# Decode attention on one core: output weights in longer rows with selection matmuls, and the last keys and values in smaller loads

## Chip, cores and metric

The kernel runs on 1 core of one Trainium2 chip. The metric is device time in microseconds (us) of one execution.

## The reference, cut to what matters

Two attention layers decode one new token for a batch of 4, and their outputs are concatenated. The model width is D = 512, and a head has 128 elements.

```python
# A: 32 query heads share 8 key/value heads; only the last W = 2048 of 8192 keys count
W = min(4096, max(256, Sk // 4))
k = jnp.repeat(k_cache[:, :, Sk - W:, :], 4, axis=1)      # v likewise
# B: 32 heads, each with its own 8192 keys
scores = einsum("bhqd,bhkd->bhqk", x @ wq, k) * Dh ** -0.5
o = einsum("bhqk,bhkd->bhqd", softmax(scores), v)
out = o.reshape(B, 1, 32 * 128) @ wo
return concatenate([a, b], axis=-1)
```

The caches are what costs: 32 MB of them are read for A (8 chunks of 2 MB of keys and 2 MB of values), 512 MB for B. Each element is used once, so this is a problem of loading.

## The kernel before

Work is cut into chunks. An A chunk is one key/value head for all four batches: 2 MB of keys and 2 MB of values. There are 8 of them. A B chunk is two heads of one batch: 4 MB and 4 MB, and there are 64. PE (the matmul engine) transposes the keys in groups of 8 tiles, multiplies them with the queries, and in the next chunk multiplies the values with the softmax weights. The DVE (vector) and ACT (scalar) engines copy the transposed keys out of PSUM, the memory into which PE writes, and do the softmax in between.

```python
def keys_part(c):
    for g in range(ch["NG"]):                 # 8 groups in A, 16 in B
        emit_T(ch["s"] + g)                   # 8 transposes, then a copy to SBUF on DVE or ACT
        if g >= SLAG:
            emit_S(ch["s"] + g - SLAG)        # scores, two groups behind
        if 1 <= c < NCA and g == 2: stats_gmax(c - 1)     # softmax of the chunk before:
        if 1 <= c < NCA and g == 3: stats_exp(c - 1)      # max, shift, exp, row sums
        if 1 <= c < NCA and g == 6: norm_sum(c - 1)
        if 2 <= c < NCA and g == 4: emit_fin(c - 2)       # output projection of A
        ...
        if c >= NCA and c % 2 == 1 and g == 10: emit_fin(ahead(c, 2))   # of B
```

One queue issues the loads in the order of use. A load waits for the buffer that it fills. The output weights of a group of heads are loaded with one weight row of 512 elements (1 KB) per descriptor.

```python
def dma_wo(g):                                # A: 512 KB per chunk, 8 of them
    src = A_wo[g * 4 * P:(g + 1) * 4 * P, :].rearrange("(hl d) n -> d hl n", d=P)
    ...
def dma_wos(hp):                              # B: 256 KB per head pair, 16 of them
    src = B_wo[2 * hp * P:2 * (hp + 1) * P, :].rearrange("(hl d) n -> d hl n", d=P)
```

## Time and profile before

| | before |
|---|---|
| time, three runs | 1381.89 us median (1379.97 to 1385.78) |
| profiled run | 1380.14 us, span 1378.3 us |
| PE busy | 1174.6 us (85%) |
| DVE busy, ACT busy | 641.7 us (47%), 436.0 us (32%) |
| DMA | 587.53 MB, mean 426 GB/s |
| packets under 2 KB | 10992 of 30085 |

The DMA engines have work from the first slice of the span to the last, and PE is busy 85% of it, over three stages: A (from about 34 us, when the first scores are done, to about 116 us), B (to 1352 us) and a tail without loads that matter. The distance between two landings is what a load costs the stream, and the distance between two like instructions of successive chunks (the chunk period) is what a chunk costs the engines. The period in A, read from the starts of the first softmax instruction of each chunk (the group `sA<-sc,mk`), is 11.16 us before. The stream of loads is read from the landings of A's weights, one load per chunk: they are 11.27 to 11.32 us apart (about 4.9 us for the keys, 4.95 for the values and 1.44 for the weights). So these two are within 0.15 us of each other.

### The profile page before, as it was taken

How to read it: one execution, taken by the hardware profiler on the slowest of the kernel's cores; microseconds unless marked ns; L12 is line 12 of the kernel's file. 1: busy time of each engine (PE TensorE's matmuls, PEld its weight loads, DVE VectorE, ACT ScalarE, POOL GpSimd, SP SyncE). 2: the span in 40 equal slices, each digit the busy share in tenths (PEclk: the TensorE clock that was granted, in tenths of full speed). 3: DMA queues.
4: the chain of work that ended last, by engine and by line, in shares of the span. 5: the costliest groups of instructions: out<-in, count | busy, mean ns of one | idle time of the engine just before them, and what ended most of it. 6: DMA issues, size and time to landing. Idle time of an engine off the chain costs nothing.

```text
span 1378.3 us, 59408 instructions
## 1 busy us (share of the span) xinstructions
PE 1174.6 (85%) x26901; PEld 1132.8 (82%) x26901; DVE 641.7 (47%) x1337; ACT 436.0 (32%) x649; POOL 4.8 (0%) x18
## 2 busy tenths in 40 slices
PE   4887898888888888888889888988898888888988
PEld 4776898888888887888888888888898888888987
DVE  1665454444444444444444444444454445444543
ACT  1553233323223322332233232322333233332332
POOL 1000000000000000000000000000000000000000
PEclk9999999999999999999999999999999999999998
DMA  9999999999999999999999999999999999999997
GB/s 400 414 417 425 428 432 429 431 432 430 433 430 434 428 432 431 431 432 430 432 429 433 431 432 432 430 430 432 431 431 433 428 433 432 431 431 431 430 431 315
DMA packets 30085, 587.53 MB, mean 426 GB/s; under 512 B 2784, under 2 KB 10992, under 8 KB 11248
## 3 DMA queue, kind: packets, MB, share of 16 engines
q1 hardware_dynamic: 30040, 587.22, 99.6%
q8 instruction: 16, 0.26, 0.1%
q14 instruction: 5, 0.04, 0.0%
q10 hardware_dynamic: 24, 0.01, 0.0%
HBM read 587.21 MB, written 0.01 MB: 426 GB/s over the span
## 4 chain that ended last, share of the span: by engine, by line
DMA 60%; PE 37%; DVE 1%; issue 1%; ACT 0%; SPq 0%; DVEq 0%; ACTq 0%
DMA kv<-in_B_k_cache_dram 58%; PE tr L375 23%; PE sc L377 10%; PE po L377 3%; DMA kv<-in_B_wq_dram 2%; PE fin L377 2%; PE ms L377 1%; DVE sA L488 1%; DVE kt L439 0%; DVE sA L486 0%; ACT pba L551 0%; PE ms L375 0%; SPq L330 0%; SPq L314 0%; ACT kt L437 0%
## 5 line engine op out<-in xcount | busy, mean ns | idle before, releaser
L375 PE MATMUL tr<-identb,kv 128*128 128x128 bf16 x8704 | 703.5, 232 | 160.6 <-DMA kv<-in_B_k_cache_dram 158.2
L439 DVE COPY kt<-tr 128x1024 bf16<-128x1024 bf16 x736 | 503.5, 691 | 469.6 <-PE tr L375 468.6
L375 PEld LDWEIGHTS tr<-identb,kv 128*128 128x128 bf16 x8704 | 559.2, 105 | 185.7 <-DMA kv<-in_B_k_cache_dram 103.5
L437 ACT ACTIVATE kt<-tr 128x1024 bf16<-128x1024 bf16 x352 | 360.2, 1024 | 629.8 <-PE tr L375 628.9
L377 PE MATMUL sc<-qb,kt 128*128 128x64 bf16 x8704 | 446.9, 196 | 10.6 <-DVE kt L439 10.3
L377 PEld LDWEIGHTS sc<-qb,kt 128*128 128x128 bf16 x8704 | 369.3, 100 | 14.5 <-DVE kt L439 11.6
L377 PE MATMUL po<-pbb,kv 128*128 128x64 bf16 (+1 forms) x8320 | 293.8, 191 | 7.0 <-issue 7.0
L377 PEld LDWEIGHTS po<-pbb,kv 128*128 128x128 bf16 x8320 | 266.8, 97 | 9.1 <-issue 7.3
L536 ACT ACTIVATE pbb<-sc,negb 64x128 bf16<-64x128 f32 x128 | 51.2, 400 | 295.2 <-DVE negb L526 294.4
L502 DVE TENSOR_REDUCE rm<-sc 64x1 f32<-64x128 f32 x128 | 37.0, 289 | 93.1 <-PE sc L377 92.2
L514 DVE TENSOR_REDUCE gm<-ms 1x2 f32<-1x128 f32 (+1 forms) x72 | 20.1, 279 | 44.5 <-PE ms L375 44.4
L526 DVE COPY negb<-ms 128x1 f32<-128x1 f32 (+1 forms) x72 | 11.4, 159 | 55.4 <-PE ms L377 55.4
L377 PE MATMUL ms<-identf,gx 1*128 1x1 f32 (+1 forms) x144 | 27.2, 256 | 0.0
L377 PEld LDWEIGHTS ms<-identf,gx 1*128 1x128 f32 (+1 forms) x144 | 21.1, 182 | 4.5 <-DVE gx L518 0.4
L536 ACT ACTIVATION_READ_ACCUMULATOR pbb<-sc,negb 64x1 f32 x128 | 23.7, 185 | 0.0
L375 PE MATMUL ms<-identf,rm 128*1 128x128 f32 (+1 forms) x72 | 19.5, 271 | 2.3 <-DVE rm L497 2.3
L377 PE MATMUL po<-pba,kv 128*128 128x64 bf16 x512 | 20.1, 199 | 0.5 <-ACT pba L551 0.5
L377 PE MATMUL fin<-wos,oz 128*4 128x512 bf16 x66 | 20.0, 385 | 0.3 <-DVE oz L616 0.3
L377 PEld LDWEIGHTS po<-pba,kv 128*128 128x128 bf16 x512 | 17.9, 102 | 0.6 <-ACT pba L551 0.6
L518 DVE TENSOR_SCALAR gx<-gm 1x128 f32<-1x128 f32 (+1 forms) x72 | 15.9, 221 | 2.7 <-DVE gm L514 0.2
L377 PE MATMUL ms<-xT,kv 128*128 128x4 bf16 x256 | 7.1, 166 | 8.5 <-DMA kv<-in_A_wq_dram 4.4
L377 PEld LDWEIGHTS ms<-xT,kv 128*128 128x128 bf16 x256 | 7.0, 104 | 8.7 <-DMA kv<-in_A_wq_dram 4.5
(46 smaller groups left out, 136.0 us busy)
## 6 DMA issues: line engine op xcount, KB each, us to landing
kv<-in_B_k_cache_dram SPq DMA_DIRECT2D x64, 4096.0 KB, 27.3
kv<-in_B_v_cache_dram SPq DMA_DIRECT2D x63, 4096.0 KB, 32.0
kv<-in_A_k_cache_dram SPq DMA_DIRECT2D x8, 2048.0 KB, 14.0
kv<-in_A_v_cache_dram SPq DMA_DIRECT2D x8, 2048.0 KB, 16.2
kv<-in_A_wq_dram SPq DMA_DIRECT2D x1, 4096.0 KB, 12.3
kv<-in_B_wq_dram SPq DMA_DIRECT2D x1, 4096.0 KB, 27.2
wor<-in_A_wo_dram SPq DMA_DIRECT2D x8, 512.0 KB, 11.3
wos<-in_B_wo_dram SPq DMA_DIRECT2D x16, 256.0 KB, 20.8
```

The costliest lines, as they stand in the source:

```text
L375: sch.add("pe", lambda e: e.transpose(o, l, r), waits, key)
L377: sch.add("pe", lambda e: e.matmul(o, l, r, start=start, stop=stop), waits, key)
L437: sch.add("act", lambda e: e.activation(dst, src, ACTF.Copy), waits=waits, key=("ev", s))
L439: sch.add("dve", lambda e: e.tensor_copy(dst, src), waits=waits, key=("ev", s))
L488: emit = lambda e, src=src, b=b: e.scalar_tensor_tensor(out=t, in0=src, scalar=mk[:, b:b + 1], in1=t, op0=ALU.mult, op1=ALU.add)
L502: sch.add("dve", lambda e, src=src, pp=pp: e.tensor_reduce(out=rm[pp, m, 0:1], in_=src, axis=AX.X, op=ALU.max), waits=[("S", ch["s_last"]) ...
L514: sch.add("dve", lambda e: e.tensor_reduce(out=gm[0:C, m, 0:U], in_=src, axis=AX.X, op=ALU.max), waits=[("trm", c)], key=("gmax", c))
L518: sch.add("dve", lambda e: e.tensor_scalar(out=dst, in0=gv, scalar1=-scale, scalar2=None, op0=ALU.mult), waits=[("gmax", c)], key=("gx", c))
L526: sch.add("dve", lambda e: e.tensor_copy(negb[:, m, 0:C], ms[:, col:col + C]), waits=[("bc", c)], key=("negb", c))
L536: sch.add("act", lambda e, src=src, pp=pp, n=n, u=u: e.activation(pbv[pp, :, u], src, ACTF.Exp, bias=negb[pp, m, 0:1], scale=scale, accum_ ...
```

## The change

The intent has two parts. First, fewer short packets: a partition takes four (A) or two (B) neighbouring weight rows as one row of 4 or 2 KB. The rows then lie in another order than the attention output, so the output is permuted by selection matmuls and copied before the projection. Second, a shorter tail: the last keys come in two halves, so that PE can start on the first, and the last value pieces are smaller. For the last chunk the weights are turned back by a matmul, so that no selection stands in the tail.

```diff
-LASTV = (64, 32, 16, 16)
+LASTV = (64, 32, 16, 8, 8)
 ...                                  # dma_wo (A); dma_wos (B) likewise with r=2
-            src = A_wo[...].rearrange("(hl d) n -> d hl n", d=P)
+            src = A_wo[...].rearrange("(p r) n -> p (r n)", r=4)
 ...                                  # last keys in halves
+            if kind == "k" and c == NC - 1:
+                x = slice(0, NTB // 2 * P), slice(NTB // 2 * P, NTB * P)
+                sch.add_dma("sp", ... dst[:, x[0]], src[:, x[0]] ..., key=(kind, c))
+                sch.add_dma("sp", ... dst[:, x[1]], src[:, x[1]] ..., key="kl")
 ...                                  # emit_T: the second half is awaited in mid-chunk
+                    if c >= NCA and c % 2 == 1 and g == NTB // TG // 2:
+                        waits += [("wos2", ahead(c, 2))]
 ...                                  # last values with 64 columns
-                n = NW if c < NC - 1 else UC
+                n = NW
 ...                                  # the selection: k = 4 in A, 2 in B
+        def emit_sel(c):
+            for r in range(k):
+                pe_mm(ms[:, Z0 + r * n:...], sel[:, r, :], x, waits=[("oT", c)] + ms_read ...)
+            for h in range(k):
+                sch.add("dve", ... tensor_copy(z[pp, :]..., src), waits=[("sm", c)] + free ...)
+            ms_read[:] = [("z", c)]
 ...                                  # keys_part
                 if 2 <= c < NCA and g == 4:
+                    emit_sel(c - 2)
+                if 2 <= c < NCA and g == 7:
                     emit_fin(c - 2)
+                if c >= NCA and c % 2 == 1 and g == 8:
+                    emit_sel(ahead(c, 2))
 ...                                  # before the last values
         norm_sum(NC - 1)
+        emit_wol()                    # 4 matmuls with 512 columns, two copies
```

In `keys_part`, A's projection goes from the fifth group to the eighth, to leave time for the selection. At the end of A (`finish_A`, not shown) two selections are put in, and one projection is moved behind the exponential there too.

More of the change, by code (lines that the diff above doesn't have):

```diff
@@ L22 @@
 NW = 64
-LASTV = (64, 32, 16, 16)
+LASTV = (64, 32, 16, 8, 8)
 TRM0, BC0, L0, Q0, XT0 = 0, 256, 288, 320, 448
+Z0 = Q0
 class _Record:
@@ L240, in bass_concat_heads__sliding_block_cached__mha_block_cached__decode_kernel @@
         outsb = sb("outsb", [36, DO], BF16)
+        sel4 = sb("sel4", [P, 4, P], BF16)
+        sel2 = sb("sel2", [P, 2, P], BF16)
+        back2 = sb("back2", [P, 2, 2, P], BF16)
+        zA = sb("zA", [P, 2, 16], BF16)
+        zB = sb("zB", [P, 8], BF16)
+        wol = sb("wol", [P, 2, DO], BF16)
         tr = ps("tr", [P, NTRB, TG * P], BF16)
@@ L249, in bass_concat_heads__sliding_block_cached__mha_block_cached__decode_kernel @@
         semnames += ["d_h%d" % i for i in range(NH)] + ["d_vl%d" % i for i in range(len(LASTV))]
-        semnames += ["d_wo%d" % i for i in range(NWO)] + ["d_wos"]
+        semnames += ["d_wo%d" % i for i in range(NWO)] + ["d_wos", "d_kl"]
         sems = {n: es.enter_context(nc.semaphore(n)) for n in semnames}
@@ L274, in bass_concat_heads__sliding_block_cached__mha_block_cached__decode_kernel @@
         sch.add("pool", lambda e: e.memset(pbt[1][:, :, :], 0.0), key=("c_pb", 1))
+        for r in range(4):
+            sch.add("pool", lambda e, r=r: e.affine_select(
+                out=sel4[:, r, :], in_=onesb[:, :], pattern=[[0, 4], [-4, 32]], compare_op=ALU.is_equal,
+                fill=0.0, base=-r, channel_multiplier=1), waits=["c_onesb"])
+        for r in range(2):
+            sch.add("pool", lambda e, r=r: e.affine_select(
+                out=sel2[:, r, :], in_=onesb[:, :], pattern=[[0, 2], [-2, 64]], compare_op=ALU.is_equal,
+                fill=0.0, base=-r, channel_multiplier=1))
+            for u in range(2):
+                sch.add("pool", lambda e, r=r, u=u: e.affine_select(
+                    out=back2[:, u, r, :], in_=onesb[:, :], pattern=[[1, P]], compare_op=ALU.is_equal,
+                    fill=0.0, base=P * u - r, channel_multiplier=-2), key="c_sel" if r == u == 1 else None)
         half_of = {}
@@ L304, in dma_wo @@
         def dma_wo(g):
-            src = A_wo[g * 4 * P:(g + 1) * 4 * P, :].rearrange("(hl d) n -> d hl n", d=P)
+            src = A_wo[g * 4 * P:(g + 1) * 4 * P, :].rearrange("(p r) n -> p (r n)", r=4)
             slot = wo_slot(g)
-            dst = wor[:, slot, :].rearrange("p (hl n) -> p hl n", hl=4)
+            dst = wor[:, slot, :]
             sch.add_dma("sp", lambda e: e.dma_start(dst, src), "d_wo%d" % slot,
@@ L311, in dma_wos @@
         def dma_wos(hp):
-            src = B_wo[2 * hp * P:2 * (hp + 1) * P, :].rearrange("(hl d) n -> d hl n", d=P)
-            sch.add_dma("sp", lambda e: e.dma_start(wos[:, :, :], src), "d_wos",
+            src = B_wo[2 * hp * P:2 * (hp + 1) * P, :].rearrange("(p r) n -> p (r n)", r=2)
+            sch.add_dma("sp", lambda e: e.dma_start(wos[:, :, :].rearrange("p r n -> p (r n)"), src), "d_wos",
                         waits=[("fin", NCA + 4 * hp - 1)] if hp else [], key=("wos", hp))
@@ L341, in dma_kv @@
                 return
+            if kind == "k" and c == NC - 1:
+                x = slice(0, NTB // 2 * P), slice(NTB // 2 * P, NTB * P)
+                sch.add_dma("sp", lambda e: e.dma_start(dst[:, x[0]], src[:, x[0]]), "d_h%d" % at, waits=waits, key=(kind, c))
+                sch.add_dma("sp", lambda e: e.dma_start(dst[:, x[1]], src[:, x[1]]), "d_kl", key="kl")
+                return
             sch.add_dma("sp", lambda e: e.dma_start(dst, src), "d_h%d" % at, waits=waits, key=(kind, c))
@@ L361, in bass_concat_heads__sliding_block_cached__mha_block_cached__decode_kernel @@
                 hp = max(0, c - NCA - 2) // 4
-                sch.add("sp", lambda e: e.sem_inc(sems["eng_sp"], 1), waits=[("wos", hp)],
+                sch.add("sp", lambda e: e.sem_inc(sems["eng_sp"], 1), waits=[("wos", hp)] + (["kl"] if c == NC - 1 else []),
                         key=("wos2", c - 2 if c > NCA + 1 else NONE), self_inc=True)
@@ L417, in tile_of, with ahead @@
             return flat(at, chunks[c]["NT"] // NTA)[:, j * P:(j + 1) * P]
+        def ahead(c, n):
+            return c - n if c - n >= NCA else NONE
         bank_used = [None] * NTRB
@@ L614, in norm_out, with emit_wol @@
                 i1 = rz[:, :].rearrange("p (x y) -> p x y", x=2)
-            waits = [("rinv" if 0 <= c < NCA else "rz", c), ("pv", c)] + ([("fin", c - 2 if c != NCA + 1 else NONE)] if c >= 2 else [])
+            waits = [("rinv" if 0 <= c < NCA else "rz", c), ("pv", c)] + ([("sm", c - 2 if c != NCA + 1 else NONE)] if c >= 2 else [])
             sch.add("dve", lambda e: e.tensor_tensor(out=o, in0=i0, in1=i1, op=ALU.mult), waits=waits, key=("oT", c))
             po_read[:] = [("oT", c)]
+        def emit_sel(c):
+            if 0 <= c < NCA:
+                sel, x, n, z, k = sel4, oT[:, c % NSM, :], 16, zA[:, c % 2, :], 4
+                free = [("fin", c - 2)] if c >= 2 else []
+            else:
+                sel, x, n, z, k = sel2, oz[:, :], 8, zB[:, :], 2
+                free = [("fin", c - 2 if c - 2 >= NCA else NONE)] if c != NONE else []
+            for r in range(k):
+                pe_mm(ms[:, Z0 + r * n:Z0 + (r + 1) * n], sel[:, r, :], x,
+                      waits=[("oT", c)] + ms_read if r == 0 else [], key=("sm", c) if r == k - 1 else None)
+            for h in range(k):
+                pp = slice(h * P // k, (h + 1) * P // k)
+                src = ms[pp, Z0:Z0 + k * n].rearrange("p (r b h) -> p h r b", r=k, b=NB)[:, h]
+                sch.add("dve", lambda e, src=src, pp=pp: e.tensor_copy(z[pp, :].rearrange("p (r b) -> p r b", r=k), src),
+                        waits=[("sm", c)] + free if h == 0 else [], key=("z", c) if h == k - 1 else None)
+            ms_read[:] = [("z", c)]
+        def emit_wol():
+            for u in range(2):
+                o = tr[:, u, :].bitcast(F32)
+                for r in range(2):
+                    pe_mm(o, back2[:, u, r, :], wos[:, r, :], start=r == 0, stop=r == 1,
+                          waits=[("wos2", NC - 1)] if u == r == 0 else [], key=("back", u) if r else None)
+                if u == 0:
+                    sch.add("act", lambda e, o=o: e.activation(wol[:, 0, :], o, ACTF.Copy), waits=[("back", 0)], key=("wol", 0))
+                else:
+                    sch.add("dve", lambda e, o=o: e.tensor_copy(wol[:, 1, :], o), waits=[("back", 1)], key=("wol", 1))
         def emit_fin(c):
@@ L621, in emit_fin @@
             p0 = 0 if ab == 1 else 32
-            if ab == 1:
+            if c == NC - 1:
                 ov = oz[:, :].rearrange("p (b u) -> p b u", u=2)
-                ops = [(ov[:, :, u], wos[:, u, :]) for u in range(2)]
-                waits = [("oT", c), ("wos2", c)]
-            else:
-                w = wor[:, wo_slot(c), :].rearrange("p (hl n) -> p hl n", hl=4)
-                ov = oT[:, c % NSM, :].rearrange("p (u c) -> p u c", c=REP)
-                ops = [(ov[:, :, cc], w[:, cc, :]) for cc in range(REP)]
-                waits = [("oT", c), ("wo", c)]
+                ops = [(ov[:, :, u], wol[:, u, :]) for u in range(2)]
+                waits = [("oT", c), ("wol", 0), ("wol", 1)]
+            elif ab == 1:
+                ops = [(zB[:, r * NB:(r + 1) * NB], wos[:, r, :]) for r in range(2)]
+                waits = [("z", c), ("wos2", c)]
+            else:
+                w = wor[:, wo_slot(c), :].rearrange("p (r n) -> p r n", r=4)
+                ops = [(zA[:, c % 2, r * NB:(r + 1) * NB], w[:, r, :]) for r in range(4)]
+                waits = [("z", c), ("wo", c)]
             lastc = NC - 1 if ab == 1 else NCA - 1
@@ L644, in pv_done @@
                 norm_out(c)
-        def ahead(c, n):
-            return c - n if c - n >= NCA else NONE
         def keys_part(c):
@@ L699, in finish_A @@
             stats_gmax(NCA - 1)
+            emit_sel(NCA - 2)
+            stats_exp(NCA - 1)
             emit_fin(NCA - 2)
-            stats_exp(NCA - 1)
             norm_sum(NCA - 1)
@@ L705, in finish_A @@
             pv_done(NCA - 1)
+            emit_sel(NCA - 1)
             emit_fin(NCA - 1)
@@ L717, in bass_concat_heads__sliding_block_cached__mha_block_cached__decode_kernel @@
                 emit_q(1)
-                pe_mm(fin[0:36, :], pbt[0][:, 1, 0:36], pbt[0][:, 1, 0:DO], stop=False, waits=[("c_pb", 1)])
+                pe_mm(fin[0:36, :], pbt[0][:, 1, 0:36], pbt[0][:, 1, 0:DO], stop=False, waits=["c_sel"])
             values_part(None if c == 0 else NONE if c == NCA else c - 1, c)
```

## The prediction

> **What bounds the kernel now.** I read the page first (slices, queues, chain), then the DMA packet records and the landing times, then the chain of waits and the timeline of the last 40 us. The slices:
>
> ```profile
> PE   4887898888888888888889888988898888888988
> ...
> DMA  9999999999999999999999999999999999999997
> GB/s 400 414 417 425 428 432 429 431 432 430 433 430 434 428 432 431 431 432 430 432 429 433 431 432 432 430 430 432 431 431 433 428 433 432 431 431 431 430 431 315
> DMA packets 30085, 587.53 MB, mean 426 GB/s; under 512 B 2784, under 2 KB 10992, under 8 KB 11248
> ```
>
> The DMA engines are full from the first slice to the last; PE is not. So the span is a DMA stream of fixed bytes (587 MB, near 431 GB/s once problem B streams) plus what PE still does after the last loads. The early slices are slower, 400 to 428 GB/s: that is problem A, with most of the short rows. Of the 10992 packets under 2 KB, 8208 are of 1 KB, and 8192 of these are the output weights (8 loads of 512 KB and 16 of 256 KB).
>
> A load has landed when its semaphore has had the increments of all 16 engines. As loads follow each other without a gap, the distance of two landings is what the later one costs the stream. For loads of 128 rows, eight rows per engine, the trace gives 9.71 us for 32 KB rows, 4.89 for 16 KB, 2.47 for 8 KB and 1.23 to 1.24 for 4 KB (the last three are pieces of the last value chunk). Output weights in 1 KB rows cost 1.40 to 1.47 us per 512 KB (A) and 0.73 per 256 KB (B), and the load before a B one is late by another 0.02 to 0.03. Per packet that is 1214, 611, 309, 154 and, for 1 KB, 45 ns: about 37.8 ns per KB and 3 to 8 ns on top.
>
> The end, as the chain of waits has it:
>
> ```profile
> 1325.21 27.14 DMA kv<-in_B_k_cache_dram
> 1352.34 0.05 issue
> 1352.39 1.90 PE tr L375 x24
> ...
> 1365.21 0.70 PE po L377 x24
> ...
> 1370.82 0.38 PE ms L377 x2
> 1371.20 3.26 PE po L377 x128
> ...
> 1374.77 1.03 PE fin L377 x2
> 1375.80 0.02 issue
> 1375.82 0.68 DVE outsb L636
> ```
>
> The last keys land at 1352.34. From there to the end nothing waits for DMA: transposes and scores to 1365.21, the values of the last chunk but one with the softmax steps to 1371.20, the last values to 1374.46, projection, copy, store. The last value piece landed at 1371.89, before its 16 tiles were due (1371.20 + 112 x 0.0255 = 1374.06). So **the tail hangs on the landing of the last keys**, and two lines of the timeline show what PE did before them:
>
> ```profile
> 1349.02 0.41 PE L377 MATMUL po<-pbb,kv 128*128 128x64 bf16 x8
> ...
> 1352.39 1.90 PE L375 MATMUL tr<-identb,kv 128*128 128x128 bf16 x24 [2.96 <-DMA kv<-in_B_k_cache_dram]
> ```
>
> PE was idle for 2.96 us, then ran on half clock: the granted clock is 0.50 from 1353.35 to 1356.76, and eight transposes take 0.85 us there, 0.45 later.
>
> **The Trainium skill.** "DMA: Bandwidth & Descriptors", section "Why small descriptors are slow (HBM only)", says that each packet carries a fixed overhead of a few cycles and each descriptor a fixed amount of metadata. The trace agrees: 45 ns for 1 KB against 38 per KB in the longest rows. Its "Specifications" give 435 GB/s as the fabric's ceiling; the 431 here is next to it, so only overhead is left to gain. "TensorE: Matmul & The Clock Gate", Part 1, says that a free-running window of about 3.4 us decides on half clock after idling. The trace agrees: half-clock stretches last 3.41 us or multiples, and sorting this trace's windows by PE's idle time, those idle for over 2.1 us are followed by half clock, those idle for 1.64 to 1.84 (nine) are not. The same page, "Back-to-back issue gap", gives a floor of some 25 ns between small matmuls; the trace has 25.5 ns with 2 columns (3.26/128) and 29.2 with 64 (0.70/24).
>
> **The change, part by part.** (1) *Rows.* A's weights go from 1 KB to 4 KB rows. 128 rows of 4 KB is the very shape of the last value piece, 1.235 us: 8 x (1.44 - 1.235) = 1.6 us off the stream. B's go to 128 rows of 2 KB; between 1 and 4 KB the ladder gives about 82 ns a packet, 8 x 82 = 0.66 us, against 0.73 + 0.02: 16 x 0.09 = 1.4 us. Splitting the last keys adds 2 x 4.89 - 9.71 = 0.07, the smaller value pieces 2 x 0.66 - 1.235 = 0.08. Because the stream is full throughout, I count all of it on the path: **-2.9 us**, and every later landing moves by that.
>
> (2) *Selection.* A contiguous row holds four (or two) weight rows, so the attention output has to be permuted to match: 4 (A) or 2 (B) matmuls of 16 or 8 columns and as many DVE copies. At the durations of their neighbours (25 to 60 ns, 0.16 to 0.2 us) that is under 0.2 us of PE per pass and up to 0.8 us of DVE in A, 0.35 in B. The projection was moved two or three groups later, so these copies have over a microsecond. PE waits 158.2 us for B's keys in all, so 32 B passes do not show; in A the DMA is the limit with 9 us of loads queued. **0 us**, off the path.
>
> (3) *Last keys in halves.* The first half lands about 4.9 us before 1352.34, at 1347.4, before PE has finished at 1349.43. PE goes straight on, saves 2.96 us of idling and the 1.8 us of half clock. Eight groups at 0.68 us reach mid-chunk at 1354.9, after the second half landed. Transposes and scores then end at 1349.43 + 12.82 - 1.77 + 0.15 (selection) = 1360.6 instead of 1365.21. But the values of the last chunk but one land only at 1362.06. So the gain is cut there: 1365.21 - 1362.06 = **-3.15 us**, with a new wait of 1.5 us, too short for half clock by the sorting above.
>
> (4) *Weights turned back for the last chunk.* Four matmuls with 512 columns ahead of the last values, 0.22 us each at full clock by the clock of the transposes (0.056 per 128 columns): **+0.9 us**. The two copies lie beside the last values.
>
> (5) *64 columns instead of 2* in the last values: 128 x (29.2 - 25.5) ns = **+0.5 us**. In return PE should count as busy: the final stretch of half clock (from 1373.83) made the last two projections take 1.03 us, against 0.52 in mid-kernel: **-0.5 us**.
>
> (6) *Smaller pieces.* The last values would start at 1371.20 - 3.15 + 0.9 = 1368.95 and need the last 8 tiles at 1368.95 + 120 x 0.0292 = 1372.45; these land at about 1371.97. No wait. **0 us**, though the margin is only 0.5 us.
>
> Sum: -2.9 - 3.15 + 0.9 + 0.5 - 0.5 = -5.15. From 1381.89 that is 1376.7; I allow 0.3 for small new waits: **1377.0 us**, or 0.35% faster.
>
> **Rivals.** *The row length is hidden.* If the 1 KB packets' overhead overlaps with other packets (the records of packets sum to slightly more than the engines' time, 16.4 instead of 16.05 busy engines where B's weights pass), the rows give nothing and only the tail is left: about 1379.5. Against it: landings are distances on the stream itself, no sum of overlapping records. *The wait for values cools PE.* Two windows idle for 1.61 and 1.63 us were followed by half clock, and a new 1.5 us wait comes near. Then some 3.4 us of value matmuls run at half speed and the tail gives 1.5 us less: about 1378.5. *Selection or the moved projection starves the stream in A*: weight slots are freed some 2 us later per A chunk, and the issuing queue goes in order, so the next keys are issued later too. If the 9 us of queued loads were not enough, each of 6 chunks would lose up to 0.5 us, 3 us: about 1380. Also the mid-chunk wait stands in all odd B chunks, on a counter that follows the issue of that chunk's values (1309.07 for the chunk that starts at 1312.78): 3.7 us before even its start, so no stall. *The tail is bound by the stream*: if the last piece lands over 0.5 us later than reckoned, the end moves with it, by less than a microsecond for any error I can see in the ladder. No rival comes near 2%, which is 28 us.
>
> **Range and chances.** The terms differ by 1 to 2 us, the runs of before among themselves by 5.8 (1379.97 to 1385.78). Low: all terms, no new wait, a run like the fastest of before: 1373. High: rows hidden or PE cooled, and a slow run: 1381. Within 2% is nearly certain: 0.98; 0.01 each for faster and slower.
>
> **What would show it.** Right: landings 1.24 us apart for A's weights and 0.66 for B's; packets under 2 KB down to about 2800; PE goes from the value matmuls into the last chunk's transposes without a gap, and waits about 1.5 us ahead of the next values; a group of four matmuls from the turned weights of some 0.9 us; the last two projections near 0.52 us. Wrong: landings of the weights unchanged; a half-clock stretch inside the last chunk; DMA slices under 9 in A; PE waits at the ninth group of odd chunks or ahead of a projection.

## The result, and the profile after

The changed kernel took 1383.68 us (median of 6 runs, 1382.37 to 1386.97); the kernel before took 1380.51 us (median of 6, 1379.87 to 1385.78) over the same rounds. The ratio is 1.0019, with a 95% interval of 1.0000 to 1.0038. A ratio here is the mean time of one kernel's runs over that of the other's of the same rounds, so it is not quite the ratio of the two medians. The predicted gain of 5 us was not there, and the time lies above the 1381 us that the prediction called high. The profiled run after took 1382.37 us, span 1380.6 us, against 1378.3 us before.

The page's slices after, to be held against the ones in the prediction (a digit is a tenth of the busy share of a slice of 34.5 us):

```profile
DMA  9999999999999999999999999999999999999998
GB/s 401 421 393 402 388 439 426 432 433 428 438 430 428 433 428 438 430 429 433 428 431 436 429 433 428 431 436 432 430 432 427 436 432 430 433 426 432 437 425 349
DMA packets 25254, 587.53 MB, mean 426 GB/s; under 512 B 2817, under 2 KB 2833, under 8 KB 6289
```

The short packets are gone (10992 to 2833), but slices three to five, 69 to 173 us, fell from 417, 425 and 428 GB/s to 393, 402 and 388. Summed over the first five slices that is 79 GB/s less, times 34.5 us: 2.7 MB, or 6 us at 431 GB/s. The digits of the DMA row still say 9, because 9 stands for 90% or more, so they hide the loss. Two stretches of 10 us show it. The columns are stretch, length, busy time (and instructions) of PE, of PE's weight loads, of DVE, ACT and POOL, then granted clock, DMA share and GB/s. Before:

```profile
100.00:110.00 10.00, 8.46 (x172) 7.28 (x168) 6.93 (x18) 5.09 (x9) 0.00 (x0) 1.00 1.02 415
160.00:170.00 10.00, 6.82 (x128) 6.65 (x125) 2.93 (x8) 1.93 (x5) 0.00 (x0) 0.83 1.01 432
```

After:

```profile
100.00:110.00 10.00, 9.34 (x197) 7.93 (x194) 5.49 (x18) 5.48 (x9) 0.00 (x0) 1.00 0.79 324
160.00:170.00 10.00, 9.66 (x244) 9.05 (x242) 5.52 (x11) 3.61 (x4) 0.00 (x0) 1.00 0.87 348
```

In both stretches the DMA share fell below 0.9 and PE became busier: loads now wait for buffers, and PE is what they wait for. The landing times say how far it goes. A's last chunk starts its softmax at 120.44 us instead of 112.40 us, 8.0 us later. Of these, 6.4 us are six chunks with a period longer by 1.06 us. The other 1.6 us are mostly clock, and differ from profile to profile: PE started the first chunk at half clock (12.12 us instead of 11.07, a value that e7_onekey and e8_cols have too, where A is undone), and another stretch of half clock, from 76.4 us, cost 0.5 us. The first weights of B land at 118.63 us instead of 115.46 (+3.2 us), keys of B around 180 us land 5.5 us later, and the last keys at 1356.66 us instead of 1352.34 (+4.3 us).

So the question is what lengthens an A chunk: its period is 12.22 us instead of 11.16 us. The chain of waits over one A chunk is the place to look, from the first softmax instruction of one chunk to that of the next (start, length, what). Before:

```profile
56.44 0.49 DVE sA L486
...
61.12 0.38 PE ms L377 x2
61.50 0.55 PE tr L375 x8
...
62.29 0.96 PE fin L377 x4
63.24 0.55 PE tr L375 x8
...
67.59 0.49 DVE sA L486
```

After:

```profile
58.74 0.50 DVE sA L523
...
63.42 0.39 PE ms L408 x2
...
64.03 0.44 DVE sA L581
64.49 0.42 ACT eA L585
64.94 0.43 DVE rs L592
...
66.63 0.19 DVE zA L670
...
66.87 0.40 PE ms L408 x2
...
68.02 0.95 PE fin L408 x4
...
70.95 0.50 DVE sA L523
```

Before, the chain goes down PE from the softmax matmuls (`ms`) to the end of the chunk: the projection (`fin`, 0.96 us) stands in the middle of the softmax step, and PE has something to do while DVE and ACT shift, exponentiate and sum. After, the chain leaves PE at the `ms` matmuls, goes through shift, exponential, row sums and the last of four selection copies (`zA`), and comes back to PE more than 3 us later. The projection then follows on top.

The tail after, in the chain of waits:

```profile
1333.19 33.19 DMA kv<-in_B_v_cache_dram
1366.42 0.88 PE po L408 x24
...
1372.59 0.88 PE tr L408 x4
1373.47 3.76 PE po L408 x128
1377.54 0.61 PE fin L408 x2
1378.17 0.68 DVE outsb L705
```

And in the timeline (the bracket holds PE's idle time ahead and what ended it):

```profile
1353.26 1.50 PE L406 MATMUL tr<-identb,kv 128*128 128x128 bf16 x24
...
1366.42 0.88 PE L408 MATMUL po<-pbb,kv 128*128 128x64 bf16 x24 [1.84 <-DMA kv<-in_B_v_cache_dram]
```

The chain now hangs on the landing of the last values but one (1366.38 us), no longer on that of the last keys. PE goes into the last transposes without a wait. From the landing of the last keys to the end it takes 24.0 us instead of 25.9 us. So the tail did shorten by 2.0 us, and the stream brought its last keys 4.3 us late; together that is the difference of 2.3 to 2.4 us between the two spans.

### The profile page after: what moved, and what is told of

Same layout as the page of the kernel before. It is cut to its first block, busy times and chain, and to the rows that moved or that the text cites. A ratio compares the mean times of both kernels' runs of the same rounds, so it can differ in the third digit from the quotient of the medians.

```text
span 1380.6 us, 59798 instructions
## 1 busy us (share of the span) xinstructions
PE 1175.7 (85%) x27001; PEld 1131.6 (82%) x27001; DVE 656.8 (48%) x1434; ACT 436.7 (32%) x650; POOL 7.4 (1%) x28
## 2 busy tenths in 40 slices
DMA packets 25254, 587.53 MB, mean 426 GB/s; under 512 B 2817, under 2 KB 2833, under 8 KB 6289
## 4 chain that ended last, share of the span: by engine, by line
DMA 60%; PE 35%; DVE 3%; issue 1%; ACT 1%; DVEq 0%; SPq 0%; ACTq 0%
DMA kv<-in_B_k_cache_dram 56%; PE tr L406 21%; PE sc L408 9%; PE po L408 3%; DMA kv<-in_B_v_cache_dram 2%; DMA kv<-in_B_wq_dram 2%; PE fin L408 2%; PE ms L408 1%; DVE sA L525 1%; DVE kt L476 0%; DVE zA L670 0%; DVE sA L523 0%; ACT pba L588 0%; DVE sA L581 0%; ACT eA L585 0%
## 5 line engine op out<-in xcount | busy, mean ns | idle before, releaser
L406 PEld LDWEIGHTS tr<-identb,kv 128*128 128x128 bf16 x8704 | 552.7, 104 | 182.0 <-DMA kv<-in_B_k_cache_dram 98.3
L408 PE MATMUL po<-pbb,kv 128*128 128x64 bf16 x8320 | 293.9, 192 | 6.3 <-issue 4.4
L408 PE MATMUL fin<-wos,zB 128*4 128x512 bf16 x64 | 19.0, 378 | 0.0
L523 DVE TENSOR_SCALAR sA<-sc,mk 128x256 f32<-128x256 f32 x8 | 3.9, 484 | 23.2 <-PE sc L408 23.2
```

The lines of the kernel that those rows point to most:

```text
L406: sch.add("pe", lambda e: e.transpose(o, l, r), waits, key)
L408: sch.add("pe", lambda e: e.matmul(o, l, r, start=start, stop=stop), waits, key)
L523: emit = lambda e, src=src: e.tensor_scalar(out=t, in0=src, scalar1=mk[:, 0:1], scalar2=None, op0=ALU.mult)
```

## The experiments

The theory after reading the result was that A's part of the change makes the engines' chain of an A chunk longer than the stream's 11.3 us. The rivals were that the issuing queue is held back (a weight load that waits for its slot stands ahead of the next keys), that the rows themselves give nothing, and that the tail loses what it should gain. Twelve kernels were run in three calls, each call on one chip together with 11 runs of the kernel before. The medians of the kernel before were 1380.60, 1381.13 and 1380.10 us in the three calls.

| run | what it is | median us (lowest to highest) | ratio to before (95%) | A period, us |
|---|---|---|---|---|
| e1_noA | after, A's part undone | 1377.97 (1376.71 to 1378.88) | 0.9973 (0.9958 to 0.9988) | 11.16 |
| e2_Aonly | before, A's part alone | 1387.02 (1384.88 to 1387.72) | 1.0036 (1.0021 to 1.0051) | 12.22 |
| e3_move | before, A's projection moved | 1382.59 (1381.35 to 1386.16) | 1.0012 (0.9996 to 1.0028) | 12.22 |
| e5_rowsA | before, A's rows alone | 1379.75 (1378.19 to 1384.97) | 0.9995 (0.9977 to 1.0013) | 11.16; two of 12.5 to 12.6 |
| e12_order | e3_move, weights issued later | 1384.27 (1382.76 to 1384.84) | 1.0019 (1.0003 to 1.0035) | 12.22 |
| e10_early | after, A's selection earlier | 1381.23 (1379.02 to 1383.97) | 0.9998 (0.9981 to 1.0016) | 11.80 |
| e9_act | e10_early, A's copies on ACT | 1377.58 (1375.67 to 1380.32) | 0.9971 (0.9954 to 0.9989) | 11.33 |
| e7_onekey | e1_noA, last keys in one load | 1380.00 (1378.25 to 1381.21) | 0.9987 (0.9971 to 1.0004) | 11.16 |
| e4_tail | before, tail part alone | 1378.82 (1377.57 to 1382.04) | 0.9984 (0.9968 to 0.9999) | 11.16; two of 12.59 |
| e8_cols | e1_noA, 2 columns at the end | 1377.80 (1376.87 to 1380.78) | 0.9985 (0.9967 to 1.0003) | 11.16 |
| e17_wol | e1_noA, weights turned earlier | 1379.62 (1379.46 to 1379.72) | 0.9991 (0.9975 to 1.0006) | not used |
| e18_both | e9_act, weights turned earlier | 1379.29 (1377.98 to 1381.17) | 0.9992 (0.9976 to 1.0008) | not used |

The period is the value that most of a run's A chunks have; the first chunk and single stretches at half clock differ.

### Undo A's part (e1_noA)

```diff
 # in the changed kernel: A as before; B's rows and selection, and the tail, stay
-            src = A_wo[...].rearrange("(p r) n -> p (r n)", r=4)
+            src = A_wo[...].rearrange("(hl d) n -> d hl n", d=P)
                 if 2 <= c < NCA and g == 4:
-                    emit_sel(c - 2)
-                if 2 <= c < NCA and g == 7:
                     emit_fin(c - 2)
```

> The changed kernel with problem A's part undone: A's weights in 1 KB rows, no selection, projection back in its old place; B's rows and the whole tail kept. Theory (A's added work lengthens the chain of PE and DVE per A chunk from 11.2 to 12.2 us, and the loads starve): the A chunks go back to 11.2 us, the weights of B land at 115.5 us instead of 118.6, B's keys lose their late landings, and B's rows (-1.2) and the tail (-2.0) are left: 3 to 4 us faster than before, ratio about 0.9975. Rival (the loss comes from B's selection or the mid-chunk wait at the start of B): still no faster than before, late landings between 150 and 181 us remain.

It took 0.9973 of the time before, 0.27% or 3.7 us less, and less than the changed kernel, whose ratio is 1.0019. The result is correct. The A period is back at 11.16 us. So the loss lies in A's part, and what is left of the change gains.

One thing went otherwise than in the changed kernel: the wait for the last values but one is longer, as the timeline of this run shows.

```profile
1360.64 1.46 PE L408 MATMUL po<-pbb,kv 128*128 128x64 bf16 x24 [3.04 <-DMA kv<-in_B_v_cache_dram]
```

PE idled for 3.04 us, and the granted clock was half from 1360.16 to 1363.58 us: these 24 matmuls took 1.46 us instead of 0.88. From the landing to the end of the span it is 15.55 us here and 14.25 us in the changed kernel. That is the prediction's second rival, seen in this run and not in the profile of the changed kernel, at a cost of 1.3 us.

### A's part alone (e2_Aonly)

```diff
 # in the kernel before: A's rows, A's selection at the fifth group, A's projection at the eighth
+            src = A_wo[...].rearrange("(p r) n -> p (r n)", r=4)
                 if 2 <= c < NCA and g == 4:
+                    emit_sel(c - 2)
+                if 2 <= c < NCA and g == 7:
                     emit_fin(c - 2)
```

> The kernel before with problem A's part alone: 4 KB rows, selection, projection moved to the eighth group. Theory: A chunks take 12.2 us, the start of B is late, 4.5 to 6 us slower than before, ratio about 1.004. Rival (B's part at fault): 1.6 us faster from the rows, ratio 0.999.

It took 1.0036 of the time before, 5.0 us more, with a period of 12.22 us. Together with e1_noA this places the loss in A's part from both sides: taking it out gains, putting it in alone loses.

### The move of the projection alone (e3_move)

```diff
-                if 2 <= c < NCA and g == 4:
+                if 2 <= c < NCA and g == 7:
                     emit_fin(c - 2)
```

> The kernel before with A's projection moved from the fifth to the eighth group and nothing else. Theory (selection's copies on DVE are the main cost, the move a smaller one): A chunks take 11.2 to 11.7 us, 0 to 2.5 us slower. Rival (the later projection frees the weight slot late, so that the in-order issuing queue sends the next keys late): A chunks take about 12.2 us and 4 to 6 us are lost, as with the whole A part.

No row and no selection is changed here, only the place of A's projection. The period is 12.22 us, so the move alone has the whole 1.06 us. The theory of this run, that the copies are the main cost, was wrong; the period is the rival's, and whether the rival's mechanism is behind it is the question of the next run. The run is slower by 0.12% or 1.7 us, with an interval that just includes no change (0.9996 to 1.0028). The chain of waits of this run over one A chunk:

```profile
57.58 0.49 DVE sA L486
...
62.26 0.39 PE ms L377 x2
...
62.87 0.44 DVE sA L544
63.33 0.43 ACT eA L548
...
63.78 1.70 ACT pba L551 x4
65.48 0.92 ACT kt L437
...
66.85 0.96 PE fin L377 x4
...
69.79 0.50 DVE sA L486
```

The chain leaves PE at 62.65 us again and comes back at 66.45 us, this time through ACT: exponential 0.43 us, four copies of the softmax weights 1.70 us, and only then the transposed keys that PE waits for (`kt`, 0.92 us). The projection of 0.96 us is added after it. Before, it stood inside that gap and cost nothing. An instruction that fills a wait of its engine is free only where it stands.

The period does not tell the whole loss: with the same period, all of A's part (e2_Aonly) cost 5.0 us. The intervals overlap, but the traces show a second place, the end of A, where selections stand too. From the start of the softmax of A's last chunk to that of B's first chunk (`rm<-sc`) it takes 27.2 us before and 27.4 us in e3_move, but 28.1 us in the changed kernel and 29.2 us in e2_Aonly, where half clock also lasted longer there (13.65 us against 6.83 us in the other three). In the last two PE waits there twice for selection copies (`zA`), 0.81 us each, at 124.89 and 133.02 us in the changed kernel. No run takes this place apart.

### The queue's order (e12_order)

```diff
 # in e3_move: an A weight load goes behind the next keys, where its slot is free
-            if kind == "v" and c < NCA:
-                dma_wo(c)
+            if kind == "k" and 2 <= c < NCA:
+                dma_wo(c - 2)
+            if kind == "v" and c == NCA - 1:
+                dma_wo(NCA - 2)
+                dma_wo(NCA - 1)
```

> The late projection alone (as in e3_move), but A's weights issued after the next keys instead of ahead of them, so that the issuing queue never holds the keys back for a projection. Theory (the late projection lengthens the chain of PE and DVE itself): A chunks still take 12.2 us and the time stays within 1 us of e3_move, ratio about 1.001. Rival (keys issued late): A chunks go back to 11.2 us and the time to that of the kernel before.

The weights can no longer hold the keys back, and the period stays at 12.22 us. The ratio is 1.0019, not better than that of e3_move. So the queue's order is not the cause. This agrees with PE's waits in A: from 36 us on, PE waits for A's keys for 0.5 us in all in the kernel before, and never in the changed kernel, in e3_move or in e12_order.

### A's rows alone (e5_rowsA)

```diff
 # in the kernel before; the products are wrong on purpose, the work is the same
-            src = A_wo[...].rearrange("(hl d) n -> d hl n", d=P)
+            src = A_wo[...].rearrange("(p r) n -> p (r n)", r=4)
```

> The kernel before with A's weights loaded in 4 KB rows and used as if they were in the old order; the result of the A half is wrong on purpose. It gives the rows without their cost. If the A stage is bound by the loads, each weight lands in 1.24 instead of 1.44 us and 1.6 us are gained, ratio 0.9988. If the A stage is paced by PE and DVE at 11.16 us per chunk, the loads get shorter but the gain is under 0.5 us, since the next loads are issued no earlier.

The result is wrong (relative error 0.93): the weights come in 4 KB rows and are used in the old order. The ratio is 0.9995, no measurable gain, but the interval (0.9977 to 1.0013) holds both of the expectations. In its trace the first weights of B landed at 113.53 us, 1.9 us before those of the kernel before (115.46 us), so the rows do shorten the stream in A: A's weights landed 11.03 to 11.07 us apart. But the keys that were issued at 139.93 us, 4.0 us later than before (135.95 us), landed at 155.86 us, as before (155.85 us): their buffer came free late, and the gain was gone. This profile also had two stretches at half clock in A, at 84.1 and 108.0 us, and A's last chunk began 3.2 us later than before. So this one trace does not show what the rows would give without them, and whether the 1.6 us can be had stays open.

### The selection earlier, the projection back (e10_early) and the copies on ACT (e9_act)

```diff
 # e10_early, in the changed kernel
-                if 2 <= c < NCA and g == 4:
+                if 2 <= c < NCA and g == 1:
                     emit_sel(c - 2)
-                if 2 <= c < NCA and g == 7:
+                if 2 <= c < NCA and g == 4:
                     emit_fin(c - 2)
 # e9_act, in addition, for A's four copies
-                sch.add("dve", ... e.tensor_copy(zo, src) ...)
+                sch.add("act", ... e.activation(zo, src, ACTF.Copy) ...)
```

> The changed kernel with A's selection at the second group and its projection back at the fifth; copies still on DVE. Theory (the late place of the projection was most of the 1.06 us per A chunk): A chunks take 11.2 to 11.7 us, the copies (4 x 0.18 us) on DVE cost at most 0.7 us each, total 0 to 3 us faster than before, ratio 0.998 to 1.0. Rival (the DVE copies are the cost wherever they stand): A chunks stay near 12.2 us and the time at that of the changed kernel, ratio 1.002.

> As e10_early, with A's four selection copies on ACT, which idles about 1.9 us after its first eviction of an A chunk. If the copies on DVE cost anything, this is faster than e10_early and A chunks are at 11.2 us; the time then equals e1_noA (ratio 0.997) or is up to 1 us better. If ACT's evictions are held up instead, A chunks stay over 11.5 us.

With the projection back in its place, the period is 11.80 us: 0.64 us are left for the selection. Its four copies now stand on DVE ahead of PE's next matmul into the same PSUM tile (in the chain of waits of one chunk the last copy, `zA`, ends at 61.09 us and the `ms` matmul starts at 61.13 us). With the copies on ACT the period is 11.33 us, 0.17 us above the kernel before; so 0.47 us of the 0.64 are the copies on DVE. The chain of waits of e9_act:

```profile
58.41 0.49 DVE sA L523
...
61.23 0.26 PE ms L408 x4
...
64.43 0.96 PE fin L408 x4
...
69.74 0.50 DVE sA L523
```

The chain stays on PE from the selection (`ms`, four matmuls, 0.26 us) on, as before the change, and no copy stands in it. The times follow: 0.9998 for e10_early and 0.9971 for e9_act. The second is faster than both the kernel before and the changed kernel, keeps all parts of the change, and is correct. It is not better than e1_noA (0.9973), which has A's old rows. So these runs measure no gain from A's rows even where their selection is nearly free; a gain of 1.6 us would be 0.0012 of the time, less than the half width of either interval.

### The last keys in one load (e7_onekey)

```diff
 # in e1_noA
-            if kind == "k" and c == NC - 1:
+            if False and kind == "k" and c == NC - 1:
-                ... waits=[("wos", hp)] + (["kl"] if c == NC - 1 else [])
+                ... waits=[("wos", hp)]
```

> e1_noA with the last keys in one load again. Theory (prediction's term of 3.15 us): PE idles about 3 us ahead of the last transposes and runs them at half clock, the wait for the last values but one goes, and the time is 3 us over e1_noA, ratio to before about 0.9995. Rival (the tail is bound by the landing of the values anyway): within 1 us of e1_noA.

The ratio is 0.9987, against 0.9973 of e1_noA, which ran in another call; the intervals overlap. That is 1.9 us where 3 were expected. The traces are clearer: PE waits 2.88 us for the last keys and runs on half clock after it, as in the kernel before, and from their landing at 1350.97 us to the end of the span it is 26.9 us. The kernel before has 25.9 us for that. The sum of the prediction's terms that are left gives 25.9 + 0.9 (turned weights) + 0.5 (columns) - 0.4 (projections at full clock) = 26.9 us. So the halves do what they were meant to do. In spans e1_noA is 1.7 us shorter (1376.2 against 1377.9), and would be some 1.3 us shorter still without its half clock.

### The tail alone (e4_tail)

```diff
 # in the kernel before: pieces (64, 32, 16, 8, 8), halves, 64 columns; no turned weights
```

> The kernel before with the tail part alone: last keys in halves, 64 columns in the last values, last pieces of 8; no long rows, no selection, no turned weights. Prediction's terms: -3.15 for the halves, +0.5 for the columns, -0.5 for the projections at full clock, then held by the landing of the last piece: 2.0 to 3.0 us faster, ratio about 0.998; where the new wait for values brings half clock, 1.4 us less. Rival (the tail gains nothing by itself, e1_noA is fast by its rows): within 1 us of before.

The ratio is 0.9984, a gain of 2.2 us, with an interval that ends just below 1. The profiled run was the slowest of its six (1382.04 us): half clock at 85.2 and 109.1 us inside A, with two chunks of A at 12.59 us, and again at the wait for the last values but one. That trace is not typical of the runs, and no term is read from it.

### Two columns at the end (e8_cols)

```diff
 # in e1_noA
-                n = NW
+                n = NW if c < NC - 1 else UC
```

> e1_noA with 2 columns in the last values instead of 64. Prediction's terms: the last values take 3.26 us instead of 3.76, the last two projections 1.03 instead of 0.61: within 0.3 us of e1_noA, ratio to before 0.997. Rival: the columns only cost, and it is 0.5 us faster.

The last values take 3.33 us instead of 3.76 in e1_noA. The granted clock falls to half from 1369.09 us, and the last two projections take 1.03 us instead of 0.61. The sums are 4.36 and 4.37 us: in this pair of profiles, wider matmuls in the last values cost what they save by keeping up the clock. The ratio, 0.9985, is not told apart from that of e1_noA.

### The weights turned earlier (e17_wol, e18_both)

```diff
 # in e1_noA (e17_wol) and in e9_act (e18_both): into the wait for the last values but one
         norm_sum(NC - 1)
-        emit_wol()
 ...
+            if c == NC - 1:
+                emit_wol()
             values_part(None if c == 0 else NONE if c == NCA else c - 1, c)
```

> e1_noA with the turned weights made ahead of the last values but one, in PE's new wait, instead of after them. If that wait is real, the 0.88 us of four matmuls leave the path and the wait is shorter, so that half clock comes less often: 1 to 2 us faster than e1_noA, ratio to before about 0.9963. Against it: the last pair of chunks leaves the loop and its instructions have to be fetched, and the landing of the last piece holds it: no faster than e1_noA.

> e9_act with the turned weights made as in e17_wol. As e17_wol: ratio to before about 0.996 if the two add up, 0.997 if the turned weights give nothing.

This was to hide 0.9 us of PE in a wait, and it failed: 0.9991 and 0.9992, no better than e1_noA and e9_act. The trace of e17_wol shows where it went. The engines run B's chunks in a loop over like pairs. With four more matmuls the last pair is no longer like the others, leaves the loop, and its instructions are fetched while they are needed: seven fetches of 16 KB between 1338 and 1374 us, each one packet of 1.02 to 1.11 us, where e1_noA has one fetch. At 1347.04 us PE had been idle for 1.94 us without waiting for anything that the profile shows, and half clock followed until 1350.52 us. So the wait in which the four matmuls were to hide was gone: they started at 1362.28 us, after the values had landed (1362.02 us). The trace of e18_both shows the same (idle for 2.25 us, matmuls at 1361.65 us, landing at 1360.67 us). Loads came later too. The first half of the last keys landed 5.85 us after the load before it, where such a load otherwise takes 4.89 us, and the last value piece cost 1.08 us instead of 0.63 us. A fetch runs during the first of these (from 1344.63 us) and just ahead of the second (from 1370.07 us); that the fetches held them up is inferred from these times. In e18_both, with fetches at like times, only one load lost much (10.28 us instead of 9.7). PE also shows 0.74 us of issue time in the middle of the last values.

## Why the prediction was wrong

The step that failed is part (2): "in A the DMA is the limit with 9 us of loads queued" and, drawn from it, "0 us, off the path". The page supports that for the span as a whole, but in A the engines' chain took 11.16 us per chunk and the stream 11.3 us. They were nearly level, and no more than about 0.1 us could be added to the chain for free. The cost of selection was counted as busy time of PE and DVE, and the chain of waits of one A chunk was never read. It would have shown that PE is the chain from the softmax matmuls on, and that the projection stands in a gap of PE. Moving it cost 1.06 us per chunk (e3_move), which is the 0.96 us of the projection and a little more. The selection costs 0.64 us per chunk with its copies on DVE where the projection stays (e10_early); in the changed kernel the two do not add up, as its period of 12.22 us is that of the move alone. Over six A chunks this adds up to 6.4 us, in the profile to 8.0 us with the half clock. The queued loads took up a part: keys around 180 us landed 5.5 us late, and B's longer rows won back 1.2 us, which leaves the 4.3 us of the last keys. The 9 us of queued loads only delay the moment at which a late PE is felt: after it the stream waits for buffers that PE frees late (DMA share 0.79 from 100 to 110 us).

The third rival ("selection or the moved projection starves the stream in A") named the right place, and its time of about 1380 was nearer than the main line. Its mechanism, the order of the issuing queue, is refuted by e12_order. The first rival, that the row length is hidden, is refuted by the landings of part (1). The fourth did not come: the last piece landed at 1376.28 us, 0.7 us before its tiles were due (1373.47 + 120 x 0.0292 = 1376.97).

Part (1), rows: the landings came as predicted, 1.24 to 1.29 us for A's weights where the stream did not wait, and 0.64 to 0.68 for B's. For B the sum holds: from the landing of its first weights to that of the load ahead of its last ones e1_noA took 1225.24 us and the kernel before 1226.43 us, 1.2 us less where 1.4 was predicted. For A no run shows the 1.6 us in the time: e5_rowsA brought the stream forward by 1.9 us at the end of A, and it was given back by 155.86 us. That they are never on the path is not shown.

Parts (3) to (6), the tail: the predicted sum is -3.15 + 0.9 + 0.5 - 0.5 = -2.25 us, and the time from the landing of the last keys to the end fell by 2.0 us. The wait for the values is 1.84 us (predicted 1.5), the turned weights take 0.88 us (0.9), the last values 3.76 us (3.74), the projections 0.61 us (0.52), and the last small pieces cost 0.63 us each (0.66). The second rival, half clock at the wait, is absent in this profile and present in e1_noA (a wait of 3.04 us) and e4_tail (3.18 us). The prediction's sorting, by which a wait of 1.5 us was too short for half clock, does not hold up: see the last section.

With A's term taken out, the prediction's sum is -5.15 + 1.6 = -3.55 us. e1_noA, which is just that, gained 3.7 us. So apart from A the working was right, though the closeness is partly luck: the interval is 1.7 to 5.8 us, and this profile holds 1.3 us of half clock that the sum leaves out. A's part was off by some 7 to 8 us: predicted to gain 1.6 us, it costs 6.4 us (the ratio after, 1.0019, less that of e1_noA, 0.9973, times 1381; the two ran in different calls) or 5.0 us (e2_Aonly). The starting point, 1381.89 us from three runs, was 1.4 us above the median of six (1380.51 us), which hides some of the miss in the absolute time.

One of the signs that the prediction named was too coarse. "DMA slices under 9 in A" did not come, though A was starved: the digit 9 covers everything from 90% up over 34.5 us. The GB/s row below it showed the loss. And every sign of being right came (the landings, 2833 short packets, no gap ahead of the last transposes, a wait of 1.84 us, matmuls of 0.88 us), because all of them stand in the rows and the tail. None of them watched the period of A's chunks. One sign of being wrong did come, once: at the end of A, PE waited 0.8 us for a selection copy ahead of a projection.

What stays open is the spread between runs of one kernel, mostly 2 to 7 us. Seven of the fourteen profiles show a stretch at half clock between 55 and 115 us, inside A (one in the changed kernel, e2_Aonly, e3_move and e10_early, two in e4_tail, e5_rowsA and e17_wol), and in the last three A chunks with such a stretch took about 12.6 us. That this makes the slower runs slow is not shown: the profiled run of e4_tail was the slowest of its six, but that of e5_rowsA, also with two stretches, the second fastest.

## What to carry to other kernels

Before work is called off the path in a stage, compare in that stage the period of the engines' chain with the demand of the stream; when they are level, queued loads only delay the loss. An instruction that fills its engine's gap must be moved with the gap in mind: here, moving 0.96 us of matmuls by three groups cost over 1 us per chunk, and putting the projection back and the new copies on the engine with room (ACT) brought most of it back. A change that breaks the likeness of loop bodies near the end can cost more in instruction fetches than it saves. And signs that are to tell right from wrong should cover the parts counted as free.

## What the Trainium skill lacked or had wrong

- "TensorE: Matmul & The Clock Gate", Part 1, gives half clock after at least one idle window of about 3.4 us. Here a partly idle one was enough. All fourteen traces were cut into windows of 3.41 us, in step with the starts of their half-clock stretches, from 45 us on. Of the windows at full clock, all 453 in which PE was idle for more than 2.0 us in all were followed by half clock. Of the 202 with 1.5 to 2.0 us, 71 were; of the 4089 with less, only six.
- These six (0.40 to 0.94 us idle) stand near the end of the six kernels whose last values have 2 columns, one in each; none of the eight whose last values have 64 has one. So how wide the matmuls are matters too, of which that part says nothing. In e8_cols the clock fell to half from 1369.09 us and the last two projections took 1.03 us; with 64 columns in e1_noA it did not, and they took 0.61 us.
- "DMA: Bandwidth & Descriptors", Specifications, gives 512 bytes as the smallest transfer at line rate. Here 1 KB packets took 45 ns, 8 KB packets 309 and 32 KB packets 1214, which is 45, 39 and 38 ns per KB, so a sixth of the rate was still missing at 1 KB.
- "Runtime: NRT & Kernel Launch", Instruction fetch mechanics, says that instructions are refilled in blocks of 16 KiB and calls crossing such a boundary mostly hidden. In e17_wol, whose DMA engines are full, it was not: each fetch took 1.02 to 1.11 us, and seven of them in the last 40 us went with 1.94 us in which PE stood idle without a wait and with a load of 5.85 us instead of 4.89. The page warns of a stall after a branch, but not of what fetches cost the loads.
